# Storing eight of 85 rows in blocks of 5, 121 and 2 partitions

## The chip, the cores and the metric

The kernel runs on one core of a Trainium2 chip. A core has TensorE (PE), VectorE (DVE), ScalarE (ACT), GpSimd (POOL) and SyncE (SP), and 16 DMA engines that move data between the chip's main memory and the on-chip memory of 128 partitions. The metric is the device time in microseconds of one execution.

## The reference

The input `x` is 384 x 384 positions of 384 channels in bfloat16, 113.2 MB. The kernel averages each channel over all positions, multiplies by one weight, takes the sigmoid and scales every channel of `x` by it:

```python
g = jnp.einsum("bhwc->bc", x) / (H * W)
s = _sigmoid(g * w1d[0])          # k = 1: no neighbours, no padding
return x * s[:, None, None, :]
```

[...]

## The kernel before

The 147,456 positions are laid out as 1,152 rows for each of the 128 partitions; a row is 384 channels, 768 bytes in a partition. The on-chip tile `arena` holds 275 rows. 368 of the 1,152 rows are kept on the chip through the first pass: 72 as they are, and 296 as groups in which four rows are packed into the room of three. They form the chunk `KEPT`. The other 784 rows, with one that stays in `arena`, form the chunk `STREAMED` and are read a second time after the sum is complete.

In the first pass TensorE sums the rows as they land, and DVE and ACT pack the groups (`fold`). Then ACT computes the sigmoid into `s_bf`. In the second pass DVE, at first with GpSimd beside it, multiplies rows by `s_bf` (`scale`, `scale_both`), unpacks the groups (`unfold`), and the rows go out; space that comes free takes the next streamed rows.

Every transfer of data is issued by SyncE, from `load` (L240) and `store` (L469). `Flow.add` records each step with the rows that it reads and writes, and works out what it has to wait for; `Flow.emit` writes the steps out in the order in which they were recorded and puts waits ahead of them. Each DMA gets a semaphore of its own from a ring of 24 for each engine. A load into rows of `arena` waits until all stores that read these rows have landed. SyncE works in order, so what is behind a waiting transfer on it waits too.

The order of loads and stores in the second pass comes out of a planner, the `while True` loop at the end of the kernel's function. It steps a clock by 0.05 us, with assumed costs of rows (`ROW`, `PER_LOAD`, `PER_STORE`), and calls `scale`, `load` and `store` when its model says so. Multiplied rows go through the list `waiting`; when their time comes, one store is recorded for them:

```python
        while waiting and waiting[0][0] <= now:
            _, n, then, chunk, a, lo, known = waiting.popleft()
            known.append(store(chunk, a, lo, lo + n))
```

Late in the second pass the rows are taken in pieces of up to 85: four loads of 85 rows and one of 37, each multiplied by DVE in two or three instructions and stored whole. GpSimd's last work before the exit is `again`, a redo of the packed rows for values that the packing cannot hold, behind a branch on the register loaded at L570.

The last transfers on SyncE, in order: a store of 16 rows; two stores of 85 rows; two loads of 85 rows, each into the rows that one of these two stores empties; a load of 37 rows; two stores of 85 rows and one of 37. The change concerns the second of the first two stores of 85 rows. It holds the streamed rows 492 to 576 and goes out when DVE ends at 597.3 us.

Of the kernel before, what the change touches and what calls it, by code (L numbers as in the profile page):

```python
# [11 lines left out]
class Step:  # L12
    __slots__ = ("eng", "emit", "dma", "lane", "deps", "wanted", "rank", "waits", "know", "i", "block")

    def __init__(self, eng, emit, dma):
        self.eng, self.emit, self.dma = eng, emit, dma
        self.deps, self.wanted, self.rank, self.waits, self.know = [], False, 0, [], None
        self.lane, self.block = None, False


class Flow:
# [6 lines left out]
    def __init__(self, nc, tc):  # L28
# [2 lines left out]
        self.writer, self.readers = {}, {}  # L31
        self.queued = {}

    def add(self, eng, emit, reads=(), writes=(), dma=False, after=(), block=False):
        s = Step(eng, emit, dma)
        s.block = block
        s.i = len(self.steps)
        deps = set(after)
        for c in reads:
            if c in self.writer:  # L40
                deps.add(self.writer[c])
        for c in writes:
            if c in self.writer:
                deps.add(self.writer[c])
            for r in self.readers.get(c, ()):
                deps.add(r)
        if dma:
            q = self.queued.setdefault(eng, [])
            s.lane = (eng, len(q) % self.LANES)
            s.rank = len(q) // self.LANES + 1  # L50
            if len(q) >= self.LANES:
                deps.add(q[-self.LANES])
            q.append(s)
        for d in deps:
            if d.eng == eng and not d.dma and not dma:

                if eng == "PE":
                    continue
            s.deps.append(d)
        for c in writes:  # L60
            self.writer[c] = s
            self.readers[c] = []
        for c in reads:
            if c not in writes:
                self.readers.setdefault(c, []).append(s)
        self.steps.append(s)
        return s

    def emit(self):
        nc = self.nc  # L70
        engines = {"SP": nc.sync, "ACT": nc.scalar, "PE": nc.tensor, "DVE": nc.vector, "POOL": nc.gpsimd}

        know = {e: {} for e in engines}

        def covers(k, d):
            return k.get(d.lane, 0) >= d.rank if d.dma else k.get(d.eng, -1) >= d.i

        for s in self.steps:
            k = know[s.eng]
            for d in sorted(s.deps, key=lambda d: -d.i):  # L80
                if covers(k, d):
                    continue
                s.waits.append(d)
                d.wanted = True
                for key, v in d.know.items():
                    if k.get(key, -1) < v:
                        k[key] = v
            s.know = dict(k)
            if s.dma:
                s.know[s.lane] = s.rank  # L90
            else:
                s.know[s.eng] = s.i

        count, sems = {}, {}
        for s in self.steps:
            if not s.dma and s.wanted:
                s.rank = count[s.eng] = count.get(s.eng, 0) + 1

        def sem(s):
            key = s.lane if s.dma else s.eng  # L100
            if key not in sems:
                name = f"f_{key[0]}{key[1]}" if s.dma else f"f_{key}"
                sems[key] = self.tc.alloc_semaphore(name)
            return sems[key]

        last = {}
        with self.tc.tile_critical(sync_engine=mybir.EngineType.Pool, no_gpsimd_drain=True):  # L107
            for s in self.steps:
                eng = engines[s.eng]
                waits = [(sem(d), d.rank * (16 if d.dma else 1)) for d in s.waits]  # L110
                hold = None if s.dma or not waits else waits.pop()
                for h, v in waits:
                    eng.wait_ge(h, v)  # L113
                if s.block and hold:
                    eng.wait_ge(*hold)
                    hold = None
                ins = s.emit()
                if ins is None:
                    continue
                if hold:  # L120
                    ins = ins._wait_ge(*hold)
                if s.dma:
                    ins.then_inc(sem(s), 16)
                    last[s.lane] = s
                elif s.wanted:
                    ins.then_inc(sem(s), 1)
            for lane, s in sorted(last.items(), key=lambda at: at[1].i):
                engines[lane[0]].wait_ge(sem(s), 16 * s.rank)


# [1 line left out]
def kernel(  # L132
# [11 lines left out]
    nc = tc.nc  # L144
    P = nc.NUM_PARTITIONS
# [46 lines left out]
    arena = pool.tile([P, ROWS, C], bf16, name="arena")  # L192
# [10 lines left out]
    xf = x.rearrange("b h w c -> (b h w) c")  # L203
    of = out.rearrange("b h w c -> (b h w) c")

    def view(t, r0, n):
        return t[r0 * P : (r0 + n) * P, :].rearrange("(p r) c -> p r c", r=n)

    def rows(lo, n):
        return [("a", r) for r in range(lo, lo + n)]  # L210

    fl = Flow(nc, tc)
# [5 lines left out]
    STREAMED, KEPT = (0, N_STREAM + 1), (N_STREAM + 1, N_KEPT - 1)  # L218
    LAST_ROW = ROWS - 1
    r = 0  # L220
# [10 lines left out]


    summed = [0]

    def load(chunk, a, lo, hi):

        r0, n = chunk
        fl.add(
            "SP",
            lambda: nc.sync.dma_start(out=arena[:, a : a + hi - lo, :], in_=view(xf, r0, n)[:, lo:hi, :]),  # L240
            writes=rows(a, hi - lo), dma=True,
        )
# [53 lines left out]
    def fold(k):  # L296
# [46 lines left out]
        reads=["ones", "w_bf"], writes=["bank0"],  # L343
# [4 lines left out]
        reads=["bank0"], writes=["w_sc"],  # L348
# [38 lines left out]
    for i, bk in enumerate(banks):  # L387
        lo, hi = i * BANK, min((i + 1) * BANK, PS * C)
# [36 lines left out]
    for a, n in [(U, 8), (A, 20), (A + 20, 11), (A + 31, 8), (V, 8), (Y + 1, 6), (T + 5, 4), (T + 2, 3), (T, 2)]:  # L425
# [8 lines left out]
        reads=["bank0", "w_sc"], writes=["s_bf"],  # L434
# [30 lines left out]
    def store(chunk, a, lo, hi):  # L465
        r0, n = chunk
        return fl.add(
            "SP",
            lambda: nc.sync.dma_start(out=view(of, r0, n)[:, lo:hi, :], in_=arena[:, a : a + hi - lo, :]),  # L469
            reads=rows(a, hi - lo), dma=True,  # L470
        )
# [114 lines left out]
        return None  # L586

    written = []


    ROW, PER_LOAD, PER_STORE = 0.2267, 0.112, 0.061
# [66 lines left out]
    t = 1.0  # L658
# [58 lines left out]
    while True:  # L717
# [9 lines left out]
        if dve_at <= now:  # L727
# [4 lines left out]
            if landed and (ahead < PENDING or not can):  # L732
                chunk, a, lo, n, end = landed.popleft()
# [7 lines left out]
                if end or ahead < MERGE:  # L741
                    b, first = since
                    send(chunk, b, first, lo + n, stored(b, lo + n - first))
                    since = None
            elif can:
                f, t, then = turns.popleft()
# [5 lines left out]
        if alongside and alongside[0][0] <= now:  # L752
            _, chunk, a, lo, n = alongside.popleft()
            store(chunk, a, lo, lo + n)
            moves.append([now + LAT, n * ROW + PER_STORE, stored(a, n)])
        while waiting and waiting[0][0] <= now:
            _, n, then, chunk, a, lo, known = waiting.popleft()
            known.append(store(chunk, a, lo, lo + n))
            last_is_load = False
            moves.append([now + LAT, n * ROW + PER_STORE, then])  # L760
        if not asked and not line and not turns:
# [9 lines left out]
        if bank_at is None and len(line) <= total - BANKS_AT and got and max(got)[0] > PS * 4 // 3:  # L771
            a = max(got)[1]
# [3 lines left out]
            for i, bk in enumerate(banks):  # L776
                lo, hi = i * BANK, min((i + 1) * BANK, PS * C)
# [6 lines left out]
        if got and todo < N_STREAM:  # L784
            n, a = max(got)
            n = min(n, CAP, N_STREAM - todo)
# [57 lines left out]
```

## Time and profile before

| | |
|---|---|
| runs | 719.43, 718.50, 719.11 us; median 719.11 |
| the profiled execution | 720.44 us; its span 718.5 us |
| busy | PE 215.7, DVE 467.6, ACT 116.5, POOL 94.8 us |
| DMA | 303.68 MB in 16,860 packets, mean 423 GB/s |
| main memory | 190.32 MB read, 113.25 MB written |
| granted TensorE clock | 0.659 on the mean |

The span runs from the first instruction of the profiled execution to its last; the time of the execution holds some more on both sides. An engine is busy while it executes, so a high share does not say that it sets the end. For the 16 DMA engines the profile gives no row for each, only their mean share and the bytes that they moved, by slices of the span or by any stretch that is asked for. A packet counts in the stretch in which it starts, with its whole time and all its bytes. In the tables of stretches the columns are: the stretch and its length in us, then the busy us and the instructions of PE, PEld, DVE, ACT and POOL, the granted clock, the DMA share and GB/s.

### The profile page before, as it was taken

How to read it: one execution, taken by the hardware profiler on the slowest of the kernel's cores; microseconds unless marked ns; L12 is line 12 of the kernel's file. 1: busy time of each engine (PE TensorE's matmuls, PEld its weight loads, DVE VectorE, ACT ScalarE, POOL GpSimd, SP SyncE). 2: the span in 40 equal slices, each digit the busy share in tenths (PEclk: the TensorE clock that was granted, in tenths of full speed). 3: DMA queues.
4: the chain of work that ended last, by engine and by line, in shares of the span. 5: the costliest groups of instructions: out<-in, count | busy, mean ns of one | idle time of the engine just before them, and what ended most of it. 6: DMA issues, size and time to landing. Idle time of an engine off the chain costs nothing.

```text
span 718.5 us, 2016 instructions
## 1 busy us (share of the span) xinstructions
PE 215.7 (30%) x1202; PEld 0.3 (0%) x3; DVE 467.6 (65%) x369; ACT 116.5 (16%) x97; POOL 94.8 (13%) x40
## 2 busy tenths in 40 slices
PE   4577877999697870000000000000000000000000
PEld 0000000000000000000000000000000000000000
DVE  4600001899989849999998999969753782028910
ACT  3700001576767630020000000000000000000000
POOL 0000000000000004513422253508010000000000
PEclk9889988999899995555555555555555555555555
DMA  9999999999999979999999999999999999999996
GB/s 376 430 445 424 431 450 428 430 438 425 420 431 426 431 328 398 402 424 428 421 434 436 432 429 444 416 441 424 436 451 432 436 437 429 440 425 421 440 432 286
DMA packets 16860, 303.68 MB, mean 423 GB/s; under 512 B 1874, under 2 KB 3026, under 8 KB 5970
## 3 DMA queue, kind: packets, MB, share of 16 engines
q1 hardware_dynamic: 16848, 303.57, 98.9%
q8 instruction: 4, 0.07, 0.0%
q14 instruction: 6, 0.05, 0.0%
q10 hardware_dynamic: 2, 0.00, 0.0%
HBM read 190.32 MB, written 113.25 MB: 422 GB/s over the span
## 4 chain that ended last, share of the span: by engine, by line
DMA 55%; DVE 22%; PE 16%; ACT 1%; DVEq 1%; issue 1%; SPq 0%; POOLq 0%
DMA arena<-in_x_dram 37%; DMA out_dram<-arena 18%; PE bank L246 16%; DVE arena L446 15%; DVE arena L280 4%; DVE arena L286 3%; DVEq L107 1%; ACT arena L317 1%; SPq L240 0%; ACT s_bf L433 0%; SPq L839 0%; POOLq L107 0%; DVEq L113 0%; SPq L113 0%; POOLq L828 0%
## 5 line engine op out<-in xcount | busy, mean ns | idle before, releaser
L280 DVE TENSOR_SCALAR arena<-arena 128x1536 uint16<-128x1536 uint16 (+2 forms) x199 | 140.5, 751 | 124.1 <-DMA arena<-in_x_dram 99.6
L246 PE MATMUL bank<-arena,ones 128*128 128x384 bf16 x1151 | 207.6, 345 | 42.7 <-DMA arena<-in_x_dram 42.7
L446 POOL TENSOR_TENSOR arena<-arena,s_bf 128x1536 bf16<-128x1536 bf16 (+2 forms) x36 | 94.6, 2631 | 447.4 <-ACT bank L437 267.9
L446 DVE TENSOR_TENSOR arena<-arena,bank 128x3072 bf16<-128x3072 bf16 (+13 forms) x59 | 136.8, 2363 | 5.1 <-DMA arena<-in_x_dram 4.5
L317 ACT ACTIVATE arena<-arena 128x3072 uint16<-128x3072 uint16 (+1 forms) x38 | 102.5, 2696 | 146.0 <-DVE arena L280 146.0
L286 DVE TENSOR_TENSOR arena<-arena 128x3072 uint16<-128x3072 uint16 (+2 forms) x90 | 117.6, 1307 | 12.5 <-PE bank L246 9.6
L446 DVE TENSOR_TENSOR arena<-arena,s_bf 128x10752 bf16<-128x10752 bf16 (+4 forms) x15 | 77.1, 5194 | 73.8 <-DMA arena<-in_x_dram 63.7
L556 PE MATMUL bank<-odd,ones 128*128 128x1 bf16 x1 | 0.2, 187 | 277.3 <-DVE odd L551 277.3
L384 ACT COPY arena<-bank 128x512 uint32<-128x512 uint32 (+2 forms) x8 | 4.2, 533 | 42.6 <-DMA out_dram<-arena 42.4
L246 PE MATMUL bank<-s_bf,ones 128*128 128x384 bf16 x48 | 8.3, 326 | 0.0
L317 ACT ACTIVATION_READ_ACCUMULATOR arena<-arena 128x1 f32 x38 | 7.1, 186 | 0.0
L384 ACT COPY bank<-arena 128x512 uint32<-128x512 uint32 (+2 forms) x8 | 3.8, 528 | 0.0
L260 PE MATMUL bank<-arena,ones 128*128 128x384 bf16 x1 | 0.5, 477 | 7.0 <-DMA arena<-in_x_dram 7.0
L433 ACT ACTIVATE s_bf<-bank,w_sc 128x384 bf16<-128x384 f32 x1 | 0.6, 580 | 9.4 <-PE bank L246 9.4
L812 ACT ACT_TABLE_LOAD x1 | 1.3, 1283 | 0.7 <-PEq L828 0.7
L337 DVE MEMSET ones<- 128x128 bf16 x1 | 0.2, 165 | 1.0 <-PEq L828 1.0
L342 PE MATMUL bank<-w_bf,ones 1*128 1x1 bf16 x1 | 0.2, 179 | 2.1 <-DMA w_bf<-in_w1d_dram 2.1
L347 DVE TENSOR_SCALAR w_sc<-bank 128x1 f32<-128x1 f32 x1 | 0.2, 159 | 0.9 <-PE bank L342 0.9
L560 DVE CAST odd_i<-bank 128x1 int32<-128x1 f32 x1 | 0.2, 158 | 0.3 <-PE bank L556 0.3
L556 PEld LDWEIGHTS bank<-odd,ones 128*128 128x128 bf16 x1 | 0.1, 105 | 535.2 <-DVE odd L551 535.2
L437 ACT COPY bank<-s_bf 128x192 uint32<-128x192 uint32 x1 | 0.3, 323 | 0.0
L384 ACT COPY arena<-rest 128x64 uint32<-128x64 uint32 x1 | 0.2, 244 | 0.0
(10 smaller groups left out, 1.4 us busy)
## 6 DMA issues: line engine op xcount, KB each, us to landing
arena<-in_x_dram SPq DMA_DIRECT2D x4, 8160.0 KB, 38.4
out_dram<-arena SPq DMA_DIRECT2D x4, 8160.0 KB, 27.8
arena<-in_x_dram SPq DMA_DIRECT2D x6, 3072.0 KB, 19.7
out_dram<-arena SPq DMA_DIRECT2D x6, 3072.0 KB, 24.2
arena<-in_x_dram SPq DMA_DIRECT2D x4, 3840.0 KB, 24.3
out_dram<-arena SPq DMA_DIRECT2D x4, 3840.0 KB, 26.1
arena<-in_x_dram SPq DMA_DIRECT2D x3, 4608.0 KB, 24.7
arena<-in_x_dram SPq DMA_DIRECT2D x2, 4992.0 KB, 23.4
```

The lines of the kernel that those rows point to most:

```text
L107: with self.tc.tile_critical(sync_engine=mybir.EngineType.Pool, no_gpsimd_drain=True):
L246: return pe.add_instruction(mybir.InstMatmult(name=nc.get_next_instruction_name(), ins=[pe.lower_ap(rhs), pe.lower_ap(ones[:])], outs=[pe. ...
L260: return nc.tensor.matmul(acc, lhsT=ones[:], rhs=arena[:, i, :], start=first, stop=last)
L280: lambda: nc.vector.tensor_scalar(out=dst, in0=src, scalar1=s0, scalar2=s1, op0=op0, op1=op1),
L286: "DVE", lambda: nc.vector.tensor_tensor(out=dst, in0=a, in1=b, op=op), reads=reads, writes=writes
L317: lambda: nc.scalar.activation(out=y, in_=y, func=ACTF.Copy, accum_out=seen[:, 2 * k + i : 2 * k + i + 1]),
L384: "ACT", lambda: nc.scalar.copy(dst.bitcast(u32), src.bitcast(u32)), reads=reads, writes=writes
L433: lambda: nc.scalar.activation(out=s_bf[:], in_=acc, func=ACTF.Sigmoid, scale=w_sc[:, 0:1]),
L437: "ACT", lambda: nc.scalar.copy(s_ps.bitcast(u32), s_bf[:].bitcast(u32)), reads=["s_bf"], writes=["bank0"]
L446: lambda: vec.tensor_tensor(out=v, in0=v, in1=s[:, None, :].to_broadcast([P, n, C]), op=Op.mult),
L556: lambda: nc.tensor.matmul(votes, lhsT=ones[:], rhs=odd[:], start=True, stop=True),
L812: nc.scalar.preload_act_table(ACTF.Sigmoid)
```

## The change

Where the store of a piece of `STREAMED` covers row 500, its first four rows and its last four are taken out. They are stored by a new function, `store_shares`, in three transfers that take both ends at once, as two blocks of four rows: partitions 121 to 125 on GpSimd, partitions 0 to 120 on GpSimd, partitions 126 and 127 on SyncE, in that order. Then the 77 rows between them go out with `store` as before. One store of the kernel covers row 500, the one described above. The planner's clock and costs are as they were, and so is the order of all other steps.

In the changed program SyncE issues the 2-partition block ahead of the 77 rows. The next load waits, as before, for the other store of 85 rows; the one after it waits for the 77 rows, SyncE's block and both GpSimd blocks. On GpSimd the two transfers stand behind `again`, and the exit behind their landing. `Flow` now allows several writers of the same rows (`part`), for `load_shares`, which nothing calls.

```diff
+    FEW, MANY = 5, 11
+    EDGE = MANY * (P // MANY)
+    SHARES = [("POOL", EDGE, EDGE + FEW), ("POOL", 0, EDGE), ("SP", EDGE + FEW, P)]
+
+    def two_blocks(t, i, n, k):
+
+        d = n - k
+        if i + 2 * d <= t.shape[1]:
+            return t[:, i : i + 2 * d, :].rearrange("p (b r) c -> p b r c", b=2)[:, :, 0:k, :]
+        return t[:, i + k - d : i + n, :].rearrange("p (b r) c -> p b r c", b=2)[:, :, d - k : d, :]
...
+    def store_shares(chunk, a, lo, n, k):
+
+        r0, m = chunk
+        sb, dr = two_blocks(arena, a, n, k), two_blocks(view(of, r0, m), lo, n, k)
+        for eng, p, q in SHARES:
+            dma = nc.gpsimd if eng == "POOL" else nc.sync
+            fl.add(
+                eng, lambda dma=dma, p=p, q=q: dma.dma_start(out=dr[p:q], in_=sb[p:q]),
+                reads=rows(a, k) + rows(a + n - k, k), dma=True,
+            )
...
+    UNEVEN_STORE, N_STORE = 500, 4
...
-            known.append(store(chunk, a, lo, lo + n))
+            k = 0
+            if chunk is STREAMED and lo <= UNEVEN_STORE < lo + n:
+                k = N_STORE
+                store_shares(chunk, a, lo, n, k)
+            known.append(store(chunk, a + k, lo + k, lo + n - k))
```

More of the change, by code (lines that the diff above doesn't have):

```diff
@@ L32, in __init__, with add @@
         self.queued = {}
-    def add(self, eng, emit, reads=(), writes=(), dma=False, after=(), block=False):
+    def add(self, eng, emit, reads=(), writes=(), dma=False, after=(), part=False, block=False):
         s = Step(eng, emit, dma)
@@ L39, in add @@
         for c in reads:
-            if c in self.writer:
-                deps.add(self.writer[c])
+            deps.update(self.writer.get(c, ()))
         for c in writes:
[L43 to L46, printed above, removed]
+            if not part:
+                deps.update(self.writer.get(c, ()))
+            deps.update(self.readers.get(c, ()))
         if dma:
@@ L60, in add @@
         for c in writes:
-            self.writer[c] = s
+            if part:
+                self.writer[c].append(s)
+                continue
+            self.writer[c] = [s]
             self.readers[c] = []
@@ L126, in emit @@
                     ins.then_inc(sem(s), 1)
-            for lane, s in sorted(last.items(), key=lambda at: at[1].i):
+            for lane, s in sorted(last.items(), key=lambda at: (at[0][0] == "POOL", at[1].i)):
                 engines[lane[0]].wait_ge(sem(s), 16 * s.rank)
@@ L233, with load_shares @@
     summed = [0]
+    FEW, MANY = 5, 11
[6 more added lines that the diff above has]
+        return t[:, i + k - d : i + n, :].rearrange("p (b r) c -> p b r c", b=2)[:, :, d - k : d, :]
+    def load_shares(chunk, a, lo, n, k):
+        r0, m = chunk
+        sb, dr = two_blocks(arena, a, n, k), two_blocks(view(xf, r0, m), lo, n, k)
+        cells = rows(a, k) + rows(a + n - k, k)
+        before = {s for c in cells for s in fl.readers.get(c, []) + fl.writer.get(c, [])}
+        for eng, p, q in SHARES:
+            dma = nc.gpsimd if eng == "POOL" else nc.sync
+            fl.add(
+                eng, lambda dma=dma, p=p, q=q: dma.dma_start(out=sb[p:q], in_=dr[p:q]),
+                writes=cells, dma=True, part=p != EDGE, after=before,
+            )
+    def store_shares(chunk, a, lo, n, k):
+        r0, m = chunk
+        sb, dr = two_blocks(arena, a, n, k), two_blocks(view(of, r0, m), lo, n, k)
+        for eng, p, q in SHARES:
+            dma = nc.gpsimd if eng == "POOL" else nc.sync
+            fl.add(
+                eng, lambda dma=dma, p=p, q=q: dma.dma_start(out=dr[p:q], in_=sb[p:q]),
+                reads=rows(a, k) + rows(a + n - k, k), dma=True,
+            )
     def load(chunk, a, lo, hi):
```

## The prediction

> **What bounds the kernel now.** I read the page first: the span, the DMA rows and the chain by engine.
>
> ```profile
> span 718.5 us, 2016 instructions
> ...
> DMA  9999999999999979999999999999999999999996
> ...
> q1 hardware_dynamic: 16848, 303.57, 98.9%
> ...
> DMA 55%; DVE 22%; PE 16%; ACT 1%; DVEq 1%; issue 1%; SPq 0%; POOLq 0%
> ```
>
> The 16 DMA engines are busy through 39 of 40 slices, and all of it is SyncE's one queue. The chain names DVE for 22%, but it only follows who woke whom; the last slice alone shows less than full DMA. So I next read the chain from 541 us on, and the busy time by stage over the same stretch.
>
> ```profile
> 541.53 38.46 DMA arena<-in_x_dram
> ...
> 580.01 17.31 DVE arena L446 x3
> ...
> 597.34 24.80 DMA out_dram<-arena
> ...
> 622.16 38.42 DMA arena<-in_x_dram
> ```
>
> ```profile
> 578.10:597.30 19.20, 0.00 (x0) 0.00 (x0) 17.29 (x3) 0.00 (x0) 0.00 (x0) 0.50 1.06 460
> 597.30:602.90 5.60, 0.00 (x0) 0.00 (x0) 0.01 (x1) 0.00 (x0) 0.00 (x0) 0.50 0.94 408
> 602.90:622.10 19.20, 0.00 (x0) 0.00 (x0) 0.00 (x0) 0.00 (x0) 0.00 (x0) 0.50 1.01 435
> 622.10:641.40 19.30, 0.00 (x0) 0.00 (x0) 0.01 (x1) 0.00 (x0) 0.00 (x0) 0.50 1.00 433
> 641.40:660.60 19.20, 0.00 (x0) 0.00 (x0) 17.29 (x3) 0.00 (x0) 0.00 (x0) 0.50 0.97 420
> 660.60:677.90 17.30, 0.00 (x0) 0.00 (x0) 17.29 (x4) 0.00 (x0) 0.00 (x0) 0.50 1.04 438
> 677.90:711.16 33.26, 0.00 (x0) 0.00 (x0) 7.54 (x3) 0.00 (x0) 0.00 (x0) 0.50 0.98 424
> ```
>
> The last two columns of the stages are the DMA share and GB/s. In the chain the store issued when DVE ends at 597.3 (the one that is changed) releases a load at 622.16. By the stages that link costs nothing: the share is 0.94 to 1.06 everywhere (a packet counts where it starts, hence values above 1). Each transfer is issued while the one ahead still runs, so an engine ends when its own bytes are through, and the kernel ends with the last engine. What matters is how evenly the sixteen end. I cut the end into stretches as long as one packet of the last store: 14,208 values of 2 bytes are 28,416 bytes per partition, 1.05 us at 27 GB/s.
>
> ```profile
> 711.16:712.21 1.05, 0.00 (x0) 0.00 (x0) 0.00 (x0) 0.00 (x0) 0.00 (x0) 0.50 1.00 433
> 712.21:713.27 1.06, 0.00 (x0) 0.00 (x0) 0.00 (x0) 0.00 (x0) 0.00 (x0) 0.50 0.38 161
> 713.27:714.32 1.05, 0.00 (x0) 0.00 (x0) 0.00 (x0) 0.00 (x0) 0.00 (x0) 0.50 0.31 135
> 714.32:715.37 1.05, 0.00 (x0) 0.00 (x0) 0.00 (x0) 0.00 (x0) 0.00 (x0) 0.50 0.06 27
> 715.37:716.43 1.06, 0.00 (x0) 0.00 (x0) 0.00 (x0) 0.00 (x0) 0.00 (x0) 0.50 0.06 27
> 715.70:715.75 0.05, 0.00 (x0) 0.00 (x0) 0.00 (x0) 0.00 (x0) 0.00 (x0) 0.50 1.32 568
> 716.43:718.50 2.07, 0.00 (x0) 0.00 (x0) 0.00 (x0) 0.00 (x0) 0.00 (x0) 0.50 0.00 0
> ```
>
> Sixteen times the share is the number of packets that start: 16, then 6, 5, 1, 1. So ten engines start their last packet before 712.21 (ending by 713.3), a sixth from the back ends by 714.3, four by 715.4, and one starts its last packet at about 715.72 and ends at 716.8. The remaining 1.7 us of the span is completion and exit. Perfect levelling would share the 13 late packets, 13 x 1.05 / 16 = 0.86 us, after about 712.7, the middle of the ends of the packets before: 713.6, or 3.2 us earlier than now. That is all that uneven shares can ever bring here.
>
> Is the group of five lasting? All transfers also run out at the end of the first pass, where the sum must be complete:
>
> ```profile
> 265.00:265.50 0.50, 0.50 (x5) 0.00 (x0) 0.00 (x0) 0.00 (x0) 0.00 (x0) 1.00 0.55 204
> 265.50:266.00 0.50, 0.50 (x5) 0.00 (x0) 0.00 (x0) 0.00 (x0) 0.00 (x0) 1.00 0.33 124
> 266.00:266.50 0.50, 0.50 (x5) 0.00 (x0) 0.00 (x0) 0.00 (x0) 0.00 (x0) 1.00 0.27 94
> ```
>
> 16 x 0.33 = 5.3 and 16 x 0.27 = 4.3: again about five engines work a microsecond longer. Two separate stretches show five late engines. Which five, by number, no view tells.
>
> **The change, part by part.** Of the 85-row store issued at 597.3, rows 0 to 3 and 81 to 84 are taken out and go as pieces of 4 rows (3,072 bytes), two for each partition: 5 partitions and 121 partitions on GpSimd, 2 on SyncE. The other 77 rows go as before.
>
> Price of a byte. Large packets move at 433 / 16 = 27.1 GB/s per engine (the 711.16 row). For 3,072-byte packets I take the stretch that holds mostly those:
>
> ```profile
> 281.42:283.46 2.04, 0.00 (x0) 0.00 (x0) 2.00 (x3) 0.00 (x0) 0.00 (x0) 0.50 1.04 418
> ```
>
> 418 / (16 x 1.04) = 25.1 GB/s, 0.122 us each. Today each engine carries 8 of the 128 partitions (16 packets start per 1.05 us), so the eight rows cost each one 8 x 6,144 / 27.1 = 1.81 us. 121 is 11 x 11 and 5 is 5 x 1; if blocks are dealt out in equal whole shares, eleven engines take 11 partitions each, the other five take one, and SyncE's two partitions fall on two engines. Then:
> - eleven engines: 22 x 0.122 = 2.69, less 1.81: +0.88 us;
> - three engines: 2 x 0.122 = 0.24, less 1.81: -1.57 us;
> - two engines: 4 x 0.122 = 0.49, less 1.81: -1.32 us.
>
> No transfer of 121 or 5 partitions stands in this trace, so the dealing is an assumption: its bounds are these shares on the right engines, and the same on the wrong ones (+0.88 for the last). I take the first, since the five against eleven of the split meets the five against eleven of the two endings above. [...]
>
> Applied to the ends: the last goes from 716.8 to between 715.2 and 715.5; the four to at most 714.1; the ten to at most 713.3 + 0.88 = 714.2; the sixth from the back, if among the eleven, to at most 714.3 + 0.88 = 715.2. So the last one stays last or is about met. Weighted over the five, (3 x 1.57 + 2 x 1.32) / 5 = 1.47 us.
>
> Added issues and waits.
>
> ```profile
> L469 SPq DMA_DIRECT2D out_dram<-arena x5: 332/344/344, 578.1 to 685.5; - x5
> ```
>
> ```profile
> 602.92 20.06 SPq L240 DMA_DIRECT2D arena<-in_x_dram  x3
> ```
>
> ```profile
> 540.82 1.64 POOL L446 TENSOR_TENSOR arena<-arena,s_bf 128x768 bf16<-128x768 bf16 x1 [17.14 <-DVE arena L286]
> ```
>
> ```profile
> L570 POOLq TENSOR_LOAD <-odd_i x1: 1094/1094/1094, 583.7 to 583.7; - x1
> ```
>
> SyncE issues one more transfer: 0.34 us at 597.3, ahead of the 77 rows. The store before it is on the engines until 602.9 (the load at 602.92 waited for its landing), so the cover is up to 5 us for late engines and less for early ones, whose end is not the last: nothing. GpSimd's queue is free after its register load, 583.7 + 1.1 = 584.8; its two transfers wait for the same DVE result at 597.3 and nothing is queued behind them on GpSimd but the exit. The added waits stand on SyncE: the load issued at 622.16 must now see four pieces landed in place of one, and the loads behind it (the last, of 37 rows) queue there too. That load is not needed on the engines before the load of 602.92 is through, about 641.4. So GpSimd's pieces may be some 40 us under way, from 597.3 to about 636, less a few us for early engines, before anybody runs dry; without that cover each late microsecond costs one. DVE is idle from 597.3 to 641.4 (the stages), so the issue meets no DVE work. How long GpSimd needs to issue a transfer is not in this trace; I take it as covered, and price the other side below.
>
> Sum: -1.47 us. The profiled execution took 720.44 us, 1.94 more than its span of 718.5; so span 717.0, that execution 719.0, and 719.11 - 1.47 = **717.6 us** from the median of the runs shown. About 0.2% (1.44 us) is what a measurement of this kernel can tell from no change, and the forecast lies just beyond it.
>
> **The rivals.**
> 1. The last engine's extra lag (1.8 us behind the four) is particular to this execution. For it: the first pass ends with no such straggler. Against: it is behind through the second pass rather than by one stall. If the late engines end together at 715.4, they go to 714.1, and the sixth decides at 714.3 to 715.2: a gain of 0.2 to 1.3 us, 717.8 to 718.9. Within 0.2%.
> 2. The change does not do what it says: the 121 partitions go 8 to an engine like 128 do, fifteen engines full and one with a single partition. Then engines 0 to 4 also carry the 5 and two of them the 2: +0.24 to +0.49 us and no relief where it counts: 719.1 to 719.6. [...] The endings of 5 and 11 engines speak against counting all sixteen alike.
> 3. Equal shares, but on the wrong five: the last gets +0.88, 720.0. Within 0.2%.
> 4. The other side: GpSimd makes its 252 pieces slowly and the load of 622.16 starves. It decides from (636 - 597.3) / 252 = 0.15 us per piece; at 0.17 they land at 640.1 and the time is some 4 us longer, 723. The nearest row, 1.09 us for one GpSimd register load, stands above that per operation, but a transfer is one instruction, not 252.
>
> **How the numbers follow.** Forecast 0.56; rivals 1 to 4: 0.15, 0.09, 0.08 and 0.12. Faster by over 0.2%: 0.56. Within: 0.15 + 0.09 + 0.08 = 0.32. Slower: 0.12. The range starts at the lowest run less the largest relief, 718.50 - 1.57 = 716.9, less 0.4 for half the spread of the three runs: 716.5. It ends at 720.0, the third rival; the fourth is left out, so the range should hold 8 to 9 times in 10.
>
> **What would show it.** Right: a second kind of DMA queue with 126 x 6,144 bytes = 0.77 MB; at the end, shares that fall from 1.00 to nothing within some 2 us in place of 4; the load after the changed store issued at 620 to 621 in place of 622.16, as the late engines finish it 1.3 to 1.6 us sooner. Wrong dealing: the same staircase of 6, 5, 1, 1, or a longer one. Starved engines: a DMA share well under 1 between 600 and 660. The prediction falls if the last packet ends no earlier than 716.8 with the span unchanged, or if the time moves while the staircase does not.

## The result and the profile after

The change made the kernel slower: 722.38 us against 719.27 us (medians of six runs each), ratio 1.0038 with a 95% interval of 1.0024 to 1.0052, so 1.7 to 3.7 us. The forecast was 717.6 us, faster. The profiled execution took 722.81 us with a span of 719.8; that is only 1.3 us more span than before, because the profiled execution of before, 720.44 us, was one of its slower ones.

The page of the changed kernel has a second DMA queue (packets, MB, share of 16 engines):

```profile
q0 software_dynamic: 224, 0.77, 0.3%
```

These are the 0.77 MB that were expected. The chain after the changed store (start, us, what):

```profile
598.23 38.94 DMA out_dram<-arena
...
637.30 25.65 DMA arena<-in_x_dram
```

The second GpSimd block, issued at 598.23, landed after 38.94 us, so the load that stood at 622.16 before is issued at 637.30. It was expected at 620 to 621. GpSimd itself was quick; its two issues together took 1.5 us:

```profile
L267 POOL DMA_DIRECT2D out_dram<-arena x2: 713/772/830, 597.5 to 598.2; - x2
```

Then the DMA share and GB/s (last two columns) of two stretches, first of the changed kernel, then of the kernel before:

```profile
615.00:620.00 5.00, 0.00 (x0) 0.00 (x0) 0.00 (x0) 0.00 (x0) 0.00 (x0) 0.50 1.01 383
620.00:625.00 5.00, 0.00 (x0) 0.00 (x0) 0.00 (x0) 0.00 (x0) 0.00 (x0) 0.50 1.00 372
```

```profile
615.00:620.00 5.00, 0.00 (x0) 0.00 (x0) 0.00 (x0) 0.00 (x0) 0.00 (x0) 0.50 1.01 431
620.00:625.00 5.00, 0.00 (x0) 0.00 (x0) 0.00 (x0) 0.00 (x0) 0.00 (x0) 0.50 0.99 431
```

This is the main finding, and the share alone hides it. The engines are as busy as before, but a busy engine moves 383 / (16 x 1.01) = 23.7 and 372 / 16 = 23.3 GB/s, not 27: the same packets take longer. At 27.1 GB/s an engine the two stretches would have moved (1.01 x 433.6 - 383) x 5 us = 275 KB and (433.6 - 372) x 5 = 308 KB more (433.6 is 16 x 27.1), which is 1.34 us of all sixteen engines. Before, the same two come to 0.06 us.

The end, cut as in the prediction:

```profile
712.21:713.27 1.06, 0.00 (x0) 0.00 (x0) 0.00 (x0) 0.00 (x0) 0.00 (x0) 0.50 0.99 429
713.27:714.32 1.05, 0.00 (x0) 0.00 (x0) 0.00 (x0) 0.00 (x0) 0.00 (x0) 0.50 1.00 433
714.32:715.37 1.05, 0.00 (x0) 0.00 (x0) 0.00 (x0) 0.00 (x0) 0.00 (x0) 0.50 0.44 189
715.37:716.43 1.06, 0.00 (x0) 0.00 (x0) 0.00 (x0) 0.00 (x0) 0.00 (x0) 0.50 0.07 27
716.43:717.48 1.05, 0.00 (x0) 0.00 (x0) 0.00 (x0) 0.00 (x0) 0.00 (x0) 0.50 0.06 27
```

All sixteen are still at work two packets later than before (share 1.00 up to 714.32 in place of 712.21). Seven (16 x 0.44) start a packet in the next stretch, then one and one. The staircase starts two stretches later and is one stretch shorter: the last packet ends at about 717.9 in place of 716.8, where the prediction named an end no earlier than 716.8 as a sign against it. Most of the sixteen are later, so the loss is not only a matter of the last one's share.

### The profile page after: what moved, and what is told of

It reads as the page before. It is cut to its first block, busy times and chain, and to the rows that moved or that the text cites. A ratio compares the mean times of both kernels' runs of the same rounds, so it can differ in the third digit from the quotient of the medians.

```text
span 719.8 us, 2023 instructions
## 1 busy us (share of the span) xinstructions
PE 214.0 (30%) x1202; PEld 0.3 (0%) x3; DVE 467.5 (65%) x369; ACT 116.5 (16%) x97; POOL 96.4 (13%) x42
## 4 chain that ended last, share of the span: by engine, by line
DMA 53%; DVE 24%; PE 16%; ACT 1%; DVEq 1%; issue 1%; SPq 0%; POOL 0%; POOLq 0%
DMA arena<-in_x_dram 35%; DMA out_dram<-arena 18%; DVE arena L482 16%; PE bank L282 16%; DVE arena L316 5%; DVE arena L322 3%; DVEq L108 1%; ACT arena L353 1%; SPq L276 0%; POOL out_dram L267 0%; ACT s_bf L469 0%; SPq L114 0%; SPq L880 0%; POOLq L108 0%; POOLq L869 0%
## 5 line engine op out<-in xcount | busy, mean ns | idle before, releaser
L267 POOL DMA_DIRECT2D out_dram<-arena x2 | 1.5, 772 | 55.2 <-DVE arena L482 55.2
## 6 DMA issues: line engine op xcount, KB each, us to landing
arena<-in_x_dram SPq DMA_DIRECT2D x3, 4608.0 KB, 26.8
arena<-in_x_dram SPq DMA_DIRECT2D x2, 4992.0 KB, 23.2
```

The lines of the kernel that those rows point to most:

```text
L267: eng, lambda dma=dma, p=p, q=q: dma.dma_start(out=dr[p:q], in_=sb[p:q]),
```

## The experiments

Three causes were open at first: the shares (the wrong engines got more), the turns (GpSimd's packets alternate with long ones of SyncE, land late and slow the load beside them), and a fixed price of the GpSimd queue. All kernels start from the changed one. Ratios are to the kernel before, run on the same chip.

**1. Even shares on GpSimd.**

```diff
-    SHARES = [("POOL", EDGE, EDGE + FEW), ("POOL", 0, EDGE), ("SP", EDGE + FEW, P)]
+    SHARES = [("POOL", 0, P)]
```

> The eight rows go out on GpSimd as one transfer over all 128 partitions: the shares of the engines are even again, the GpSimd queue stays. Theory 'turns' (GpSimd's packets take turns with SyncE's packets of 59 to 65 KB, so these stores last into the next load, and the mixture slows the packets): 8 turns of 2.4 us per engine in place of 11, so the blocks land about 622 to 627 us in place of 637, the rate around 615 to 625 us is again below 400 GB/s, and the time is 1 to 2.5 us above before. Theory 'shares' (the eleven engines that got 0.8 us more include the last one): even shares, so the time is that of before within 0.5 us. Theory 'queue' (any GpSimd transfer has a fixed price at the exit or outside the span): 2 to 3 us above before, with the rate at 615 to 625 us as before.

Measured: 719.45 against 719.55 us, ratio 1.0005 (0.9995 to 1.0015). The blocks, issued at 596.82, land 24.60 us later, the load is issued at 621.48, and nothing is slow at 615 to 625 us:

```profile
615.00:620.00 5.00, 0.00 (x0) 0.00 (x0) 0.00 (x0) 0.00 (x0) 0.00 (x0) 0.50 1.04 446
620.00:625.00 5.00, 0.00 (x0) 0.00 (x0) 0.00 (x0) 0.00 (x0) 0.00 (x0) 0.50 1.00 432
```

446 / (16 x 1.04) = 26.8 and 432 / 16 = 27.0 GB/s. A GpSimd transfer as such costs nothing here, and neither do the 24.60 us that it takes among SyncE's packets. "Queue" falls, and "turns" with it as the cause of the slow packets. Here all blocks have landed at 621.42 us; run 9 shows the same rates where they go on beside the load until 639.63.

**2. The same three blocks, all on SyncE.**

```diff
-    SHARES = [("POOL", EDGE, EDGE + FEW), ("POOL", 0, EDGE), ("SP", EDGE + FEW, P)]
+    SHARES = [("SP", EDGE, EDGE + FEW), ("SP", 0, EDGE), ("SP", EDGE + FEW, P)]
```

> The three blocks of 5, 121 and 2 partitions all go on SyncE, no GpSimd transfer. Theory 'turns' and theory 'queue': the loss of rate at 615 to 625 us is gone and the load after the store is issued at about 622 us; what is left is the dealing of shares. If SyncE's transfers start at the first engine each time, engines 0 to 4 carry 12 to 13 partitions, 5 to 10 carry 11 and 11 to 15 none: +0.8 to +1.3 us for eleven of them and -1.8 for five. So within 1.3 us of before either way, and the staircase of the end shows the dealing. Theory 'shares': the same size of loss as the change, 2 to 3 us, if the late engines are among 0 to 10.

Measured: 722.74 us, ratio 1.0050 (1.0035 to 1.0065). As slow as the change without any GpSimd transfer: the blocks are at fault, not the queue. "Turns" expected the rate back to normal at 615 to 625 us; the stretches show 400 / (16 x 1.01) = 24.8 and 402 / (16 x 1.02) = 24.6 GB/s an engine. "Shares" expected this size of loss too.

**3. The same blocks on the same engines, from a later store.**

```diff
-    UNEVEN_STORE, N_STORE = 500, 4
+    UNEVEN_STORE, N_STORE = 700, 4
```

> The same three blocks on the same engines, taken from a later store of 85 rows (issued about 678 us), behind which nothing is loaded. Theory 'turns': no load is under way, so no rate below 420 GB/s and no late load; only the dealing is left, within 0.8 us of before, or a gain of up to 1.5 us if the last engine is among the five. Theory 'shares': 2 to 3 us slower, as in the change. Theory 'queue': 2 to 3 us slower, shown after the last packet or outside the span.

Measured: 721.25 us, ratio 1.0028 (1.0016 to 1.0040). No load is under way there, and 2 us are lost all the same. That speaks again against "turns". From 685 to 710 us an engine moves 25.5 to 26.9 GB/s, so packets are less slow than in the change, and "shares" fits this run as well.

**4. Sixteen partitions on GpSimd, 112 on SyncE.** The 5 and 121 partitions of the change went out in equal whole shares (its packets are linked under "Dealing of the shares" below); estimated from that, every engine gets one and seven partitions here, and the shares are even. No view of this run shows it.

```diff
-    SHARES = [("POOL", EDGE, EDGE + FEW), ("POOL", 0, EDGE), ("SP", EDGE + FEW, P)]
+    SHARES = [("POOL", 0, 16), ("SP", 16, P)]
```

> Of the same eight rows GpSimd stores 16 partitions (one for each engine) and SyncE 112 (7 for each): even shares, one GpSimd packet per engine. Theory 'turns': one turn per engine, landed by about 605 us, the load after the store issued at about 622 us as before; the time of before within 0.7 us. Theory 'shares': the time of before. Theory 'queue': 2 to 3 us above before, since GpSimd's transfer is there at all.

Measured: 722.35 us, ratio 1.0051 (1.0031 to 1.0070). No theory had this right but "queue", which run 1 rules out. Its stretches:

```profile
600.00:605.00 5.00, 0.00 (x0) 0.00 (x0) 0.00 (x0) 0.00 (x0) 0.00 (x0) 0.50 1.10 439
615.00:620.00 5.00, 0.00 (x0) 0.00 (x0) 0.00 (x0) 0.00 (x0) 0.00 (x0) 0.50 1.02 404
620.00:625.00 5.00, 0.00 (x0) 0.00 (x0) 0.00 (x0) 0.00 (x0) 0.00 (x0) 0.50 0.94 351
```

24.9, 24.8 and 23.3 GB/s an engine. So shares that are even by this estimate are slow too. What this run shares with the change and with run 2, but not with run 1, is a block that does not span all 128 partitions. That became the theory "dealing": such a block is dealt to the engines in another way than the 128-partition transfers beside it (in the change eleven partitions to each of eleven engines, where those give eight to each of sixteen), and engines get in each other's way. The second half is a guess that no view shows.

**5. All 128 partitions on SyncE, as a transfer of its own.**

```diff
-    SHARES = [("POOL", EDGE, EDGE + FEW), ("POOL", 0, EDGE), ("SP", EDGE + FEW, P)]
+    SHARES = [("SP", 0, P)]
```

> The eight rows go on SyncE as one transfer over all 128 partitions ahead of the 77 rows: no GpSimd transfer, even shares, one more issue on SyncE, descriptors as small as in the change. Theory 'dealing' (a block that does not span the 128 partitions gives its engines other partitions than those that the long stores beside it work on, and the packets of both become slow; what follows is out of step): the time of before within 0.7 us, no stretch under 420 GB/s from 600 to 625 us. Theory 'second issue' (splitting the store on SyncE is itself what costs): 2 to 3 us above before.

Measured: 719.44 against 719.19 us, ratio 1.0005 (0.9994 to 1.0016). At 600 to 605 us:

```profile
600.00:605.00 5.00, 0.00 (x0) 0.00 (x0) 0.00 (x0) 0.00 (x0) 0.00 (x0) 0.50 1.19 511
```

511 / (16 x 1.19) = 26.8 GB/s, with the eight rows issued just ahead. Neither the split nor the one issue more costs.

**6. Two halves of 64 partitions on SyncE.** Four partitions of each half to an engine, so even shares, by the estimate of run 4; no GpSimd.

```diff
-    SHARES = [("POOL", EDGE, EDGE + FEW), ("POOL", 0, EDGE), ("SP", EDGE + FEW, P)]
+    SHARES = [("SP", 0, 64), ("SP", 64, P)]
```

> [...] Theory 'dealing': 1.5 to 3.5 us above before, with a rate below 410 GB/s at 600 to 605 and at 615 to 625 us. [...]

Measured: 721.51 us, ratio 1.0028 (1.0016 to 1.0040).

```profile
600.00:605.00 5.00, 0.00 (x0) 0.00 (x0) 0.00 (x0) 0.00 (x0) 0.00 (x0) 0.50 0.96 367
615.00:620.00 5.00, 0.00 (x0) 0.00 (x0) 0.00 (x0) 0.00 (x0) 0.00 (x0) 0.50 1.17 473
620.00:625.00 5.00, 0.00 (x0) 0.00 (x0) 0.00 (x0) 0.00 (x0) 0.00 (x0) 0.50 0.97 386
```

23.9 GB/s an engine after the halves are issued (598.88 and 599.66 us), and 25.3 and 24.9 fifteen us later. Against run 5 the blocks span fewer partitions, and there are two transfers in place of one; 2 us are lost with shares that are even by the estimate, where "shares" leaves no loss. "Dealing" holds, and by that estimate a loss does not need uneven shares. Two transfers of 128 partitions on SyncE were not tried; run 7 has two on GpSimd.

**7. Two GpSimd transfers of four rows, all 128 partitions.**

```diff
-    SHARES = [("POOL", EDGE, EDGE + FEW), ("POOL", 0, EDGE), ("SP", EDGE + FEW, P)]
+    SHARES = [("POOL", 0, 1), ("POOL", 1, 2)]
...
-                eng, lambda dma=dma, p=p, q=q: dma.dma_start(out=dr[p:q], in_=sb[p:q]),
+                eng, lambda dma=dma, p=p, q=q: dma.dma_start(out=dr[:, p], in_=sb[:, p]),
```

Here `p` selects the block of four rows, no longer the partitions.

> The eight rows go on GpSimd as two transfers of 4 rows over all 128 partitions: even shares, the usual partition for each engine, but 16 packets per engine that each wait for a SyncE packet of 2.2 to 2.4 us: landed at about 637 to 641 us, so the load after the store is issued as late as in the change. Theory 'late landing costs' : engines that finish the load before (637 us at the earliest) run dry, 1 to 3 us above before. Theory 'dealing': the late load costs little as long as the last engine has work, within 1 us of before.

Measured: 720.09 us, ratio 1.0019 (1.0007 to 1.0031). It missed its aim: the second transfer, issued at 597.87, landed after 25.93 us, where sixteen turns of 2.2 to 2.4 us would be 35 to 38, and the load was issued at 623.86. It says nothing on a late landing. But it is the control for two transfers of 128 partitions, and its packets are not slow:

```profile
615.00:620.00 5.00, 0.00 (x0) 0.00 (x0) 0.00 (x0) 0.00 (x0) 0.00 (x0) 0.50 1.05 450
```

450 / (16 x 1.05) = 26.8 GB/s an engine, and the same at 620 to 625 us. Its loss of 0.5 to 2.2 us is not explained: the span of its profiled execution, 718.2 us, is no longer than that of before. So a part of the 2 us of run 6 may belong to its second transfer; by this control, which is on GpSimd and not on SyncE, the slow packets do not.

**8. The change with one row at each end.**

```diff
-    UNEVEN_STORE, N_STORE = 500, 4
+    UNEVEN_STORE, N_STORE = 500, 1
```

> The change with one row at each end in place of four: the same blocks on the same engines, a quarter of the bytes, the same count of turns and the same late load. Theory 'shares': a quarter of the shift, 0.2 us more on the eleven engines, so within 0.5 us of before. Theory 'dealing', if it goes by bytes: about 0.8 us above before; if it is enough that engines are brought out of step: 2 to 3 us. Theory 'late landing costs': 2 to 3 us, as in the change.

Measured: 720.83 us, ratio 1.0027 (1.0015 to 1.0039). A quarter of the bytes costs 1.1 to 2.8 us, more than a quarter of the loss by the middle of the interval. It is not in proportion to the bytes. The load was issued at 621.88, where that of the change was at 637.30, so the late landing is not the reason. In its profile only the stretch at 615 to 620 us is slow, 25.2 GB/s an engine; the next has 26.7.

**9. Sixteen rows on GpSimd, all 128 partitions.**

```diff
-    SHARES = [("POOL", EDGE, EDGE + FEW), ("POOL", 0, EDGE), ("SP", EDGE + FEW, P)]
+    SHARES = [("POOL", 0, P)]
...
-    UNEVEN_STORE, N_STORE = 500, 4
+    UNEVEN_STORE, N_STORE = 500, 8
```

> Sixteen rows, eight at each end, go on GpSimd over all 128 partitions: even shares, the usual partition for each engine, but twice the packets, 16 turns with SyncE's packets if a packet stays at 6,144 bytes: landed at about 636 to 640 us, as late as in the change (637). Theory 'late landing costs': engines that end the load before at 637 run dry until the late load starts; 1 to 3 us above before. Theory 'dealing': no slow packets, and the last engine is never dry, so within 0.7 us of before.

Measured: 722.25 against 718.85 us, ratio 1.0045 (1.0032 to 1.0058). Here the landing is as late as was wanted:

```profile
596.79 42.84 DMA out_dram<-arena
...
639.70 21.82 DMA arena<-in_x_dram
```

```profile
635.00:640.00 5.00, 0.00 (x0) 0.00 (x0) 0.00 (x0) 0.00 (x0) 0.00 (x0) 0.50 0.35 151
640.00:645.00 5.00, 0.00 (x0) 0.00 (x0) 4.35 (x1) 0.00 (x0) 0.00 (x0) 0.50 1.09 418
```

The engines run dry: the share falls to 0.35, about (1 - 0.35) x 5 = 3.2 us of all sixteen. The run costs 2.3 to 4.2 us. So a late landing does have a price, and the cover ends at about 637 us. That both middles are 3.2 is chance, for the profile holds two more terms: packets are slow when the load starts late, 418 / (16 x 1.09) = 24.0 GB/s an engine; and the engines end more evenly than before. At 615 to 625 us, with GpSimd's packets beside the load, they move 27.0 and 27.1 GB/s. The change issued its load at 637.30, and from 635 to 640 us its share was 1.04: it stood at the edge and lost little by this.

The slow packets of run 9 come without any block of fewer than 128 partitions. The kernel before has some too, where its last load gives way to stores:

```profile
663.00:666.00 3.00, 0.00 (x0) 0.00 (x0) 3.00 (x1) 0.00 (x0) 0.00 (x0) 0.50 1.26 474
```

474 / (16 x 1.26) = 23.5 GB/s an engine. So such a block is one way to slow packets, not the only one.

**10 and 12. The halves, and all 128 partitions, from the later store on SyncE.**

```diff
-    SHARES = [("POOL", EDGE, EDGE + FEW), ("POOL", 0, EDGE), ("SP", EDGE + FEW, P)]
+    SHARES = [("SP", 0, 64), ("SP", 64, P)]
...
-    UNEVEN_STORE, N_STORE = 500, 4
+    UNEVEN_STORE, N_STORE = 700, 4
```

Run 12 has `[("SP", 0, P)]` in place of the two halves.

> The two halves of 64 partitions on SyncE as in the run that showed +2 us, but taken from the 85-row store issued about 678 us, behind which only stores follow. Theory 'dealing', if the blocks themselves are what is slow: about 7 engine-us of long packets while they run, 0.3 to 0.7 us above before. If being brought out of step is what costs, at the next change from stores to loads: there is none behind it, so again no more than 0.7 us, and no long packets after the blocks. Against both: 2 us above before, as at the earlier place, so that neither the place nor the next load matters.

> The control to the halves at the later place: the eight rows of the store issued about 678 us go on SyncE as one transfer over all 128 partitions. Theory 'dealing': the time of before within 0.7 us, as at the earlier place, so that the 1.8 us of the halves there are the price of how they are dealt. If any split of this later store costs (one more issue and smaller packets close to the end): 1 to 2 us above before, and the halves say nothing about dealing.

Measured: the halves 720.15 against 718.85 us, ratio 1.0025 (1.0015 to 1.0035); all 128 partitions 719.09 against 719.11 us, 0.9999 (0.9990 to 1.0008). The stretch in which the blocks go out, first of the halves, then of the whole:

```profile
685.00:690.00 5.00, 0.00 (x0) 0.00 (x0) 0.67 (x1) 0.00 (x0) 0.00 (x0) 0.50 1.03 383
```

```profile
685.00:690.00 5.00, 0.00 (x0) 0.00 (x0) 1.07 (x1) 0.00 (x0) 0.00 (x0) 0.50 1.02 429
```

23.2 against 26.3 GB/s an engine. Among stores alone the packets are slow again beside the halves, so the next load is not needed for that. The expectation of 0.3 to 0.7 us was too low: the stretch explains (1.03 x 433.6 - 383) x 5 = 318 KB, 0.7 us, of the 1.1 to 2.5 us.

**11. The GpSimd blocks in the other order.**

```diff
-    SHARES = [("POOL", EDGE, EDGE + FEW), ("POOL", 0, EDGE), ("SP", EDGE + FEW, P)]
+    SHARES = [("POOL", 0, EDGE), ("POOL", EDGE, EDGE + FEW), ("SP", EDGE + FEW, P)]
```

> [...] Theory 'dealing': the blocks and their long packets are the same, so 2 to 3.5 us above before, as the change. Theory 'shares': the last engine of the change was among the eleven; if it is now among the five its end comes 2.3 us earlier and the time is 0.5 to 1.5 us above before or better; if not, the time is that of the change.

Measured: 721.29 us, ratio 1.0035 (1.0022 to 1.0048). The loss is that of the change within the intervals. "Dealing" expects that, and so does "shares" if the engine that ends last is again not among the five relieved; which engine that was, no view tells. So this run does not part "dealing" from "shares".

Taken together, at 615 to 625 us: in the change and in runs 2, 4, 6 and 11, with blocks of fewer than 128 partitions, an engine moves 23.3 to 26.1 GB/s; before and in runs 1, 5, 7 and 9, where all transfers span 128 partitions, it moves 26.7 to 27.2. Run 8, with a quarter of the bytes, lies between. There is one profile of each run.

No version here beats the kernel before.

## Why the prediction was wrong

- **What bounds the kernel**: right. Runs 1, 5 and 12, where every transfer spans 128 partitions as before, have the time of before; the losses that the profiles show are DMA time.
- **Dealing of the shares**: right in form. The sum's +0.88 and -1.57 us take equal whole shares of 121, 5 and 2 partitions, which no trace of before shows; the trace of the change shows them. If a packet that starts where another ends is taken to be on the same engine, its packets give sixteen sequences from 590 us on, five with one GpSimd packet and eleven with eleven; none has the eight of the second rival. SyncE's two partitions are on two of the five, as two packets of 3,072 bytes on each.
- **Which five**: this step failed. The prediction took the five of the split for the five late engines because both counts are five; equal counts do not say that they are the same engines. The sequence that was last at the end of the store before (602.5 us, the others 599.4 to 601.3) got eleven packets and was last again, at 717.9; two of the five relieved were among the earliest. So the last engine got the +0.88 in place of the -1.57. By the third rival this alone gives 720.0. It is not needed for a loss, by the estimate that the shares of runs 4 and 6 are even: there the loss is as large or nearly so.
- **The price of a byte**: this step failed too, and it is the one that takes the time out of the range. The terms +0.88 and -1.57 us took the duration of a packet from stretches in which every transfer spans 128 partitions, and held it to be the same beside any other. (At that duration they were nearly right: eleven packets of 6,144 bytes at 0.234 us are 2.57, less 1.81: +0.76.) With blocks of 121, 112 or 64 partitions, stretches ran at 23 to 25 GB/s an engine in place of 27, the long packets of the other transfers included (in the change those of 65,280 bytes that start from 620 to 625 us took 2.82 us on the mean, before 2.41). That is 1.34 us of all engines in two stretches alone, where the best that the shares could bring was 1.57 for the last one. Runs 5 and 6 show it, and 10 and 12 at a second place, with run 7 for the count of transfers. The kernel's own 663 to 666 us, at 23.5 GB/s, could have told beforehand that the duration is not fixed. Why a block of fewer partitions slows the packets beside it was not shown.
- **The waits**: the cover to about 636 us was rightly placed (run 9 shows its end), but the reason for a late landing was missed. GpSimd issued in 1.5 us, against the fourth rival's 0.15 us for each of 252 pieces. Then, in the trace of the change, the eleven packets of an engine came one by one between SyncE packets of 59 to 65 KB, 2.2 to 2.4 us, but for a pair at about 620 us; on the engine that was last the eleven ran from 609 to 634 us, and all had landed at 637.17. In the change this used up the cover, and little more.
- **The range** ended at 720.0, at a price of +0.88 for wrong shares. No rival had a cost common to all engines.

Open: how the loss of the change divides between the two failed steps, for in the profile of the change the engine that ended last was not among the relieved, and of the runs no view tells it; why packets are slow again at 615 to 625 us in runs 4 and 6, whose blocks were all issued by 600.3 us (before, the sequences go from the changed store to the load behind it at 618.4 to 621.8 us); the loss of run 7, and the part of that of run 10 that its profile does not show; and why one engine is later than all others in the profiled executions of before (716.8 us) and of the change (717.9).

## What to carry to other kernels

A busy DMA share does not say that the engines move data at their usual rate (at a share of 1.00 the change moved 372 GB/s, the kernel before 431 at 0.99); divide GB/s by the share, stretch by stretch. Where transfers of 128 partitions fill all DMA engines, a store of a few rows over fewer partitions can cost more than its bytes, in this kernel even with shares that are even by the estimate: two halves of 64 partitions cost 2 us where one transfer of 128 cost nothing, though a part of that may be the price of the second transfer. And a small transfer on a second queue can be as slow as the packets that it alternates with (the change's second GpSimd block landed after 38.94 us), so ask what waits for its landing.

## What was not expected of the hardware

In the trace of the change GpSimd's transfers came as 126 packets of 6,144 bytes, two pieces in one, where SyncE's came as 3,072. A 6,144-byte packet took 0.234 us at the median on either queue. When the engines had run dry in run 9, they ended more evenly: at the end all but seven had started their last packet before 716.10 us and none started one after 717.15, so the staircase of 4 us was gone, for 3.2 us of waiting. That is one profiled execution.
